# Key rows in the jobs' slots, a fourth such slot, loads three jobs ahead, and the first half's denominators during the contraction over tokens

## The chip, the cores and the metric

The kernel runs on one core of a Trainium2 chip. The metric is the device time of one execution in microseconds (us); shown are the median and the spread of several runs, and one execution taken by the hardware profiler, from which every row of a trace comes. Engines are named as in the profile: PE (TensorE; PEld its weight loads), DVE (VectorE), ACT (ScalarE), POOL (GpSimd) and SP (SyncE, which here only issues DMAs).

## What is computed

One linear-attention block on the layer norm of x, multiplied with a SwiGLU block on x itself, for 2048 tokens and 1024 channels in float32:

```
xn  = layernorm(x)
q, k, v = split(xn @ wqkv)            # 32 heads of 32
pq, pk  = phi(q), phi(k)              # phi(t) = (t+1 if t > 0 else exp(t)) + 1e-6
kv  = einsum("bhsd,bhse->bhde", pk, v)          # contraction over tokens
z   = sum of pk over tokens
o   = einsum("bhqd,bhde->bhqe", pq, kv) / (pq . z + 1e-6)
s   = o @ wo
g   = silu((silu(x @ w1) * (x @ w3)) @ w2)      # F = 3584
out = x + s * g
```

## The kernel before, in words

**Products.** Every float32 operand is split into a high and a low part in fp32r (`split`: a cast on ACT, L93, then a subtraction on DVE, L94), and every product is three matmuls of 128x512 (`mm3`, L101 to L103). Large products are done in 2 x 2 blocks with seven block products instead of eight (`gemm`). The names of a gemm's results a, b, c, d and of its sums u, c21, c12, c22 appear in the trace with a letter for the stage: ak is a of a key gemm, cg of a gate gemm. The weights' seven operands (B11, T2, T3, T1, B21, T4, B22) are made one after another from a loaded block (`Operands.made`; subtractions in L344), each in a tile of tag "b".

**Stages.** The tokens are worked in two halves of 1024. In order: preparation and keys of half 0, its q, its 28 gate and up gemms; keys of half 1; the contraction over tokens for both halves (`row_products`); q of half 1; gate and up of half 1; then the attention's output product (tiles with s in their names) and five layers of the second SwiGLU product (tiles with B).

**Keys.** For each result block of a key gemm `key_rows.use` makes phi (two activations on ACT, L497 and L498, then a DVE instruction, L499, that also gives the row sums for z, collected in `zacc` by L520) and appends a transposition to the list `later`. `turn` transposes the block on PE (tile trk, L505), copies it to a row tile (L506) and stores it to DRAM (`y_d`, L509, POOL's queue). A pair of key blocks has four row tiles: one of tag "c" and three more in two tiles of tag "b" (L529). `sums` adds their combinations on POOL.

**Contraction.** `row_products` has seven products of four steps each. A step loads 1 MB of x rows and key rows into a "raw" tile (L560, L562), for the last product also a second operand (yy, 0.5 MB, in a job slot), which POOL subtracts (L573); it splits them into four tiles of tag "b" and issues 24 matmuls (2 parts x 4 blocks x 3; tile g). A step's load is issued two steps ahead, its splits one step ahead. `row_sums` combines the results and stores them to `g_d` (L622, POOL's queue).

**Jobs.** Work that fills gaps is written as generators. `catch_up` pops one entry of `later`, or else advances the first generator of the list `jobs` by one yield; it is called six times in a gemm and twice in a step of the contraction. `tc.issue_after(m)` places what is issued inside it behind instruction m in the queue of m's engine; it orders nothing on other engines. In a gemm the first call carries a mark on ACT alone, the others one on ACT and one on DVE. `go_on` runs a list of jobs, with the loads of the next two issued ahead (L817). A job's tile comes from tag "job" with three slots of 4 KB a partition (`job_tile`, L121).

- `next_work`, during half 0: four jobs (`prepare_next`) that normalise the rows of half 1 and store its operands, with job tiles and one tile of tag "xg" (L258), and then sums of the w2 blocks (loads, POOL and DVE sums L755 to L769, stores L776).
- `attention_work`, during q, gate and up of half 1: first `spread_z` (block-diagonal `zb` in a "b" slot, L796 to L799; `zc` by L805), the denominators of half 0 (eight jobs; load L831, four matmuls L840 each, a reciprocal, and a store to `r_d`), then for each pair of wo blocks the key-value products (loads L892 of g_d and L894, matmuls L902) and the product with wo (load L917), the quotients of half 0, the denominators of half 1, and the quotients up to token block LATE = 6. A quotient (`divide`) loads pq and the reciprocals (L865, L867), waits three yields, multiplies on DVE (L873), adds block sums, and stores to `qs_d` (L877, L878), which the output product loads (L1128).
- What is left of a job list at the end of a half is run through there, without marks.

A scheduler sets the final order on each engine; the engines' queues are in order. Pools that matter: "b" with eight slots of 4 KB a partition, "raw" with two of 8 KB, "job" with three, PSUM with eight banks.

Of the kernel before, what the change touches and what calls it, by code (L numbers as in the profile page):

```python
# [16 lines left out]
P = 128  # L17
# [5 lines left out]
def tile_linear_attention_times_swiglu(  # L23
# [74 lines left out]
    def mm3(acc, w, a, start, stop):  # L98

        (wh, wl), (ah, al) = w, a  # L100
        nc.tensor.matmul(acc, lhsT=wh, rhs=ah, start=start, stop=False, skip_group_check=True)  # L101
        nc.tensor.matmul(acc, lhsT=wh, rhs=al, start=False, stop=False, skip_group_check=True)  # L102
        nc.tensor.matmul(acc, lhsT=wl, rhs=ah, start=False, stop=stop, skip_group_check=True)  # L103

# [15 lines left out]
    def job_tile(shape, name):  # L120
        return praw.tile(shape, F32, tag="job", bufs=3, name=name)  # L121

# [98 lines left out]
    def prepare_next(i):  # L221
# [8 lines left out]
        def steps(_):  # L230
# [26 lines left out]
            keep_rows(1, i, "A22", a22)  # L257
            g = st.tile([P, 2, C], F32, tag="xg", bufs=1, name=f"xg{i}")  # L258
            nc.gpsimd.tensor_add(out=g[:, 0], in0=a21, in1=a22)
            nc.gpsimd.tensor_sub(out=g[:, 1], in0=a11, in1=a21)  # L260
            yield True
            keep_rows(1, i, "S1", g.rearrange("p n c -> p (n c)"))
            for _ in range(3):
                yield True
            nc.gpsimd.tensor_sub(out=g[:, 0], in0=g[:, 0], in1=a11)
            nc.gpsimd.tensor_sub(out=g[:, 1], in0=a12, in1=g[:, 0])
            yield True
            keep_rows(1, i, "S2", g.rearrange("p n c -> p (n c)"))
            yield True
            p_ = turn("A11", a11)  # L270
            keep("A11", p_)
            nc.scalar.copy(out=a11, in_=p_)
            yield True
            p_ = turn("A21", a21)
            nc.scalar.copy(out=a21, in_=p_)
            yield True
# [234 lines left out]
    def key_rows(h, pair):  # L511
# [12 lines left out]
        def turn(n, c, pk):  # L524
            if (c, n) == (0, 0):
                t = rows[c, n] = small(f"y00_{h}_{pair}")
            else:
                if (1 - c, 1) not in pairs:
                    pairs[1 - c, 1] = pb.tile([P, 2, C], F32, tag="b", name=f"y{c}_{h}_{pair}")  # L529
                t = rows[c, n] = pairs[1 - c, 1][:, n if c else 0]  # L530
# [17 lines left out]
    def row_products():  # L548
# [39 lines left out]
        for at, s in enumerate(steps):  # L588
# [15 lines left out]
            for e, (x_, y_) in enumerate(split_.pop(s)):  # L604
                for m in M:
                    c = slice(m * P, (m + 1) * P)
                    mm3(b[m], (x_[:, 0, c], x_[:, 1, c]), (y_[:, 0], y_[:, 1]),
                        begins and e == 0 and not onto, ends and e == 1)
                    if ends and e == 1:
                        row_sums(i, m, b[m], u, v)  # L610
                catch_up()
                yield
# [31 lines left out]
    def half(h):  # L644
# [5 lines left out]
        def run(g):  # L650
            for _ in g:
                pass
# [32 lines left out]
        else:  # L685
            side_by_side(keys(0, paired=True), keys(1, paired=True))
            for pair in range(2, ND // 2):
                run(keys(pair))
            for _ in row_products():
                pass  # L690
# [125 lines left out]

    def go_on(work):  # L817

        data = [j.load() for j in work[:2]]
        for i, j in enumerate(work):  # L820
            yield from j.steps(data[i])
            if i + 2 < len(work):
                data.append(work[i + 2].load())

# [30 lines left out]
    def divide(m, k):  # L855
# [14 lines left out]
        def steps(t):  # L870
            for _ in range(3):
                yield True
# [80 lines left out]
    def late_work():  # L953
        yield from go_on([divide(m, k) for m in range(LATE, S // (2 * P)) for k in range(ND // 2)])

    def attention_work():
        yield from spread_z()
        H0, H1 = range(NCH // 2), range(NCH // 2, NCH)
        work = [j for c in H0 for j in denominators(c)]
        for k in range(ND // 2):  # L960
# [4 lines left out]
        work += [divide(m, k) for m in range(NT * H1[0], LATE) for k in range(ND // 2)]  # L965
        yield from go_on(work)

# [321 lines left out]
```

## Time and profile before

| | us |
|---|---|
| median of 3 runs | 2396.59 (2396.53 to 2399.76) |
| profiled execution | 2399.34 |
| its span in the trace | 2397.6 |
| key gemms of half 1 | about 752 to 855 |
| contraction over tokens | about 855 to 1015 |
| q, gate and up of half 1 | about 1015 to 1673 |

The profile's page gives the busy time of each engine as a share of the span, the costliest groups of instructions, and the chain of work that ended last. Its views on the trace are groups by line and tile, waits (who waited for whose instruction, in total us, times, longest), the timeline of an engine (start, duration, engine, line, operation, out<-in, and in brackets the idle time before it with what ended it), and stretches of time with the busy time of each engine in the order PE, PEld, DVE, ACT, POOL, then the granted clock of PE, the busy share of the DMA engines and GB/s. PE's busy time is modelled from pipelined matmuls; what it lost is read from the distance between the starts of matmuls and from its waits.

### The profile page before, as it was taken

What the parts mean: (1) busy time and instruction counts of PE and PEld (TensorE: products, weight loads), DVE (VectorE), ACT (ScalarE), POOL (GpSimd) and SP (SyncE); (2) the same over time, 40 slices, a digit from 0 to 9 for tenths busy, and PEclk for the clock granted to TensorE, in tenths of its full rate; (3) what the DMA queues carried; (4) which work ended last, traced back from release to release, by engine and by line L of the source; (5) the groups of instructions that cost most, each with busy time, mean ns of one, the idle gap of its engine ahead of it and who ended that gap; (6) DMA issues with size and microseconds to landing.
All of it is one profiled execution on the core that took longest, in us unless ns stands there. A gap on an engine that the chain in (4) does not pass through costs nothing.

```text
span 2397.6 us, 30961 instructions
## 1 busy us (share of the span) xinstructions
PE 2315.7 (97%) x10368; PEld 1896.1 (79%) x10368; DVE 1772.2 (74%) x2781; ACT 919.6 (38%) x1639; POOL 751.0 (31%) x892
## 2 busy tenths in 40 slices
PE   6999999999999889999999899999999999999998
PEld 5888788888887778778888788877787888888876
DVE  8878888887887655576766677777855676767798
ACT  5555333433332444344333233223423543342433
POOL 5341534367875320211423434323321000000033
PEclk9999999999999999999999999999999999999999
DMA  6455455476669566754555555557876665766588
GB/s 237 150 171 185 152 177 185 158 227 198 220 226 355 184 195 211 241 176 141 170 169 171 186 178 184 172 166 215 268 235 210 195 208 157 234 201 187 185 262 262
DMA packets 354016, 479.70 MB, mean 200 GB/s; under 512 B 24144, under 2 KB 262736, under 8 KB 353744
## 3 DMA queue, kind: packets, MB, share of 16 engines
q1 hardware_dynamic: 316608, 359.20, 47.8%
q0 software_dynamic: 37248, 118.52, 14.7%
q8 instruction: 81, 1.33, 0.2%
q14 instruction: 79, 0.65, 0.1%
HBM read 308.81 MB, written 172.49 MB: 201 GB/s over the span
## 4 chain that ended last, share of the span: by engine, by line
PE 43%; issue 10%; DMA 7%; DVE 4%; POOL 3%; ACT 1%; SPq 0%; POOLq 0%; DVEq 0%; ACTq 0%
PE g L101 2%; PE g L102 2%; PE g L103 2%; DMA qd<-pq_d 1%; PE cB L101 1%; PE cB L103 1%; PE cB L102 1%; PE aB L101 1%; PE aB L102 1%; PE dB L101 1%; PE aB L103 1%; PE dB L103 1%; PE dB L102 1%; DMA qs_d<-qd 1%; DMA rA22B<-h_d 1%
## 5 line engine op out<-in xcount | busy, mean ns | idle before, releaser
L740 POOL DMA_DIRECT2D h_d<-sg x112 | 82.7, 739 | 272.4 <-DVE sg L736 223.5
L1056 POOL DMA_DIRECT2D u_d<-uB x32 | 17.3, 540 | 407.1 <-DVE uB L1039 381.1
L94 DVE TENSOR_TENSOR xy<-xy,xy 128x512 fp32r<-128x512 f32 x112 | 75.9, 720 | 69.5 <-ACT xy L93 69.2
L93 ACT CAST xy<-xy 128x512 fp32r<-128x512 f32 x112 | 63.9, 620 | 86.2 <-PE g L103 60.1
L102 PE MATMUL g<-xy,xy 128*128 128x512 f32 x224 | 88.5, 395 | 0.0
L103 PE MATMUL g<-xy,xy 128*128 128x512 f32 x224 | 88.1, 394 | 0.0
L101 PE MATMUL g<-xy,xy 128*128 128x512 f32 x224 | 83.0, 395 | 2.8 <-ACT xy L93 2.3
L1039 DVE TENSOR_TENSOR acc<-cB,acc 128x512 f32<-128x512 f32 x50 | 34.3, 687 | 41.0 <-PE cB L103 41.0
L509 POOL DMA_DIRECT2D y_d<-y x40 | 29.7, 751 | 102.5 <-ACT y L506 79.7
L1039 DVE TENSOR_TENSOR acc<-dB,acc 128x512 f32<-128x512 f32 x56 | 38.5, 687 | 29.8 <-PE dB L103 29.6
L877 POOL DMA_DIRECT2D qs_d<-qd x32 | 17.9, 560 | 132.2 <-DVE qd L873 122.2
L722 POOL TENSOR_TENSOR hs<-sg 128x256 f32<-128x256 f32 x56 | 57.0, 1017 | 0.0
L720 POOL TENSOR_TENSOR hs<-hs,sg 128x256 f32<-128x256 f32 x56 | 56.4, 1008 | 0.1
L723 POOL TENSOR_TENSOR hs<-sg,hs 128x256 f32<-128x256 f32 x56 | 55.5, 992 | 1.6
L873 DVE SCALAR_TENSOR_TENSOR qd<-qd 128x512 f32<-128x512 f32 x32 | 21.9, 684 | 42.4 <-DMA qd<-pq_d 42.4
L101 PEld LDWEIGHTS g<-xy,xy 128*128 128x128 f32 x224 | 42.2, 189 | 12.5 <-ACT xy L93 2.9
L719 POOL TENSOR_TENSOR hs<-sg,sg 128x256 f32<-128x256 f32 x56 | 50.0, 892 | 1.2
L698 POOL DMA_DIRECT2D pq_d<-pq x32 | 17.4, 545 | 104.7 <-DVE pq L499 104.7
L102 PEld LDWEIGHTS g<-xy,xy 128*128 128x128 f32 x224 | 42.9, 192 | 9.0
L103 PEld LDWEIGHTS g<-xy,xy 128*128 128x128 f32 x224 | 42.9, 192 | 9.0
L748 POOL DMA_DIRECT2D h_d<-hs x60 | 45.9, 766 | 3.7 <-POOL hs L723 2.1
L755 POOL TENSOR_TENSOR w<-w 128x256 f32<-128x256 f32 x28 | 26.7, 955 | 58.5 <-DMA w<-in_B_w 58.5
(5311 smaller groups left out, 8383.7 us busy)
## 6 DMA issues: line engine op xcount, KB each, us to landing
h_d<-hs POOLq DMA_DIRECT2D x60, 256.0 KB, 3.3
h_d<-sg POOLq DMA_DIRECT2D x56, 256.0 KB, 3.5
w<-in_B_w SPq DMA_DIRECT2D x56, 256.0 KB
wt_d<-w SPq DMA_DIRECT2D x28, 512.0 KB
xy<-x_d SPq DMA_DIRECT2D x28, 512.0 KB
xy<-y_d SPq DMA_DIRECT2D x28, 512.0 KB
h_d<-hs SPq DMA_DIRECT2D x52, 256.0 KB
qs_d<-qd POOLq DMA_DIRECT2D x32, 384.0 KB, 4.6
```

Source lines behind the costliest of these rows:

```text
L93: nc.scalar.copy(out=hi, in_=src)
L94: return nc.vector.tensor_sub(out=lo, in0=src, in1=hi.bitcast(F32))
L101: nc.tensor.matmul(acc, lhsT=wh, rhs=ah, start=start, stop=False, skip_group_check=True)
L102: nc.tensor.matmul(acc, lhsT=wh, rhs=al, start=False, stop=False, skip_group_check=True)
L103: nc.tensor.matmul(acc, lhsT=wl, rhs=ah, start=False, stop=stop, skip_group_check=True)
L719: e.tensor_add(out=s1, in0=a21, in1=a22)
L720: e.tensor_sub(out=s2, in0=s1, in1=a11)
L722: e.tensor_sub(out=s3, in0=a11, in1=a21)
L723: e.tensor_sub(out=s4, in0=a12, in1=s2)
L740: nc.gpsimd.dma_start(out=h_d[i][2 * h + c][:, 2 * n:4 * n + 2, k], in_=src)
L748: queue.dma_start(out=h_d[i][2 * h + c][:, 6 + 4 * e:10 + 4 * e, k], in_=o[e].rearrange("p (e s) -> p e s", s=P))
L1039: return V.tensor_add(out=c, in0=src, in1=c)
```

## The change

- Tag "job" has four slots instead of three, and the tile "xg" becomes a job tile.
- `prepare_next` transposes the block A21 earlier and has three yields less for each of its four jobs.
- The two row tiles of a key pair come from the job slots instead of tag "b".
- `spread_z` and the denominators of half 0 become a job list of their own (`first_denominators`), which is appended before `row_products` and so runs in the contraction's calls of `catch_up`.
- These calls now stand behind the last matmul of their part of the step (`mm3` returns it).
- `attention_work` begins with the key-value products, and issues the loads of the next three jobs ahead.
- `divide` waits four yields instead of three for token blocks below LATE.

The number of instructions is the same.

```diff
@@ mm3
-        nc.tensor.matmul(acc, lhsT=wl, rhs=ah, start=False, stop=stop, skip_group_check=True)
+        return nc.tensor.matmul(acc, lhsT=wl, rhs=ah, start=False, stop=stop, skip_group_check=True)
@@ job_tile
-        return praw.tile(shape, F32, tag="job", bufs=3, name=name)
+        return praw.tile(shape, F32, tag="job", bufs=4, name=name)
@@ prepare_next
-            g = st.tile([P, 2, C], F32, tag="xg", bufs=1, name=f"xg{i}")
+            g = job_tile([P, 2, C], f"xg{i}")
             nc.gpsimd.tensor_add(out=g[:, 0], in0=a21, in1=a22)
             nc.gpsimd.tensor_sub(out=g[:, 1], in0=a11, in1=a21)
             yield True
             keep_rows(1, i, "S1", g.rearrange("p n c -> p (n c)"))
-            for _ in range(3):
-                yield True
+            p_ = turn("A21", a21)
+            nc.scalar.copy(out=a21, in_=p_)
+            yield True
+            yield True
             nc.gpsimd.tensor_sub(out=g[:, 0], in0=g[:, 0], in1=a11)
             nc.gpsimd.tensor_sub(out=g[:, 1], in0=a12, in1=g[:, 0])
             yield True
             keep_rows(1, i, "S2", g.rearrange("p n c -> p (n c)"))
-            yield True
             p_ = turn("A11", a11)
             keep("A11", p_)
             nc.scalar.copy(out=a11, in_=p_)
-            yield True
-            p_ = turn("A21", a21)
-            nc.scalar.copy(out=a21, in_=p_)
             yield True
@@ key_rows.turn
-                    pairs[1 - c, 1] = pb.tile([P, 2, C], F32, tag="b", name=f"y{c}_{h}_{pair}")
+                    pairs[1 - c, 1] = job_tile([P, 2, C], f"y{c}_{h}_{pair}")
@@ row_products
-                    mm3(b[m], (x_[:, 0, c], x_[:, 1, c]), (y_[:, 0], y_[:, 1]),
-                        begins and e == 0 and not onto, ends and e == 1)
+                    last = mm3(b[m], (x_[:, 0, c], x_[:, 1, c]), (y_[:, 0], y_[:, 1]),
+                               begins and e == 0 and not onto, ends and e == 1)
                     if ends and e == 1:
                         row_sums(i, m, b[m], u, v)
-                catch_up()
+                with tc.issue_after(last.ins):
+                    catch_up()
                 yield
@@ half
+            jobs.append((first_denominators(), False))
             for _ in row_products():
                 pass
@@ go_on
-    def go_on(work):
-        data = [j.load() for j in work[:2]]
+    def go_on(work, ahead=2):
+        data = [j.load() for j in work[:ahead]]
         for i, j in enumerate(work):
             yield from j.steps(data[i])
-            if i + 2 < len(work):
-                data.append(work[i + 2].load())
+            if i + ahead < len(work):
+                data.append(work[i + ahead].load())
@@ divide.steps
-            for _ in range(3):
+            for _ in range(4 if m < LATE else 3):
                 yield True
@@
+    H0, H1 = range(NCH // 2), range(NCH // 2, NCH)
+
+    def first_denominators():
+        yield from spread_z()
+        yield from go_on([j for c in H0 for j in denominators(c)])
+
     def attention_work():
-        yield from spread_z()
-        H0, H1 = range(NCH // 2), range(NCH // 2, NCH)
-        work = [j for c in H0 for j in denominators(c)]
+        work = []
         for k in range(ND // 2):
             for e, j in enumerate(merge_wo(k)):
                 work += key_values(k + e * (ND // 2)) + [j]
         work += [divide(NT * c + g, k) for c in H0 for g in range(NT) for k in range(ND // 2)]
         work += [j for c in H1 for j in denominators(c)]
         work += [divide(m, k) for m in range(NT * H1[0], LATE) for k in range(ND // 2)]
-        yield from go_on(work)
+        yield from go_on(work, 3)
```

## The prediction

> **What bounds the kernel now.** I read the page first: the busy shares and the chain of work that ended last.
>
> ```profile
> span 2397.6 us, 30961 instructions
> PE 2315.7 (97%) x10368; PEld 1896.1 (79%) x10368; DVE 1772.2 (74%) x2781; ACT 919.6 (38%) x1639; POOL 751.0 (31%) x892
> PE 43%; issue 10%; DMA 7%; DVE 4%; POOL 3%; ACT 1%; SPq 0%; POOLq 0%; DVEq 0%; ACTq 0%
> ```
>
> TensorE is busy for 97% of the span. The change keeps all 16618 instructions of the program (the compiled queues of both kernels, counted), so it can only take away or add idle time of PE. The second view is therefore the waits of PE, one row for each pair of waiting and releasing tile (columns: total us, times, longest).
>
> ```profile
> PE trk L505 <- DVE pk L499: 11.7, 4, 6.7
> PE cg__11115 L101 <- DVE c22g__11150 L462: 6.2, 1, 6.2
> PE B11s L101 <- ACT XA11s L93: 3.7, 1, 3.7
> PE g L101 <- ACT xy L93: 2.3, 1, 2.3
> PE bk__6485 L101 <- ACT T2k__6324 L93: 2.0, 1, 2.0
> PE cg__13351 L101 <- DVE c22g__13386 L462: 1.8, 1, 1.8
> PE B21s L101 <- ACT XA12s L93: 1.7, 1, 1.7
> PE bk__6485 L103 <- DVE T2k__6324 L94: 1.1, 1, 1.1
> PE ak__6979 L101 <- ACT uk__6978 L439: 1.2, 1, 1.2
> PE aq__8368 L101 <- ACT uq__8367 L439: 0.7, 1, 0.7
> ```
>
> These ten rows add up to 32.4 us. They are the waits near the edited code: the keys of the second half, the contraction over tokens, the start of q, and the division by the denominators. That is the whole stake, 1.4% of the span; the start (0 to 75 us) and the last layers keep their order of instructions.
>
> The third view is the timeline of PE, which shows what a wait costs beyond itself (columns: start, us, engine, line, operation, idle before and its releaser).
>
> ```profile
> 757.75 0.39 PE L102 MATMUL ak__6468<-A,B11k__6258 128*128 128x512 f32 x1
> 757.98 0.39 PE L103 MATMUL ak__6468<-A,B11k__6258 128*128 128x512 f32 x1
> 760.41 0.50 PE L101 MATMUL bk__6485<-S,T2k__6324 128*128 128x512 f32 x1 [2.04 <-ACT T2k__6324 L93]
> 762.27 0.64 PE L103 MATMUL bk__6485<-S,T2k__6324 128*128 128x512 f32 x1 [1.14 <-DVE T2k__6324 L94]
> 765.70 0.49 PE L102 MATMUL bk__6485<-S,T2k__6324 128*128 128x512 f32 x1
> ...
> 825.21 0.63 PE L505 MATMUL trk<-ident,pk 128*128 128x128 f32 x4 [2.26 <-DVE pk L499]
> ...
> 1007.52 1.52 PE L101 MATMUL g<-xy,xy 128*128 128x512 f32 x4 [2.33 <-ACT xy L93]
> 1011.75 0.39 PE L103 MATMUL g<-xy,xy 128*128 128x512 f32 x1
> ```
>
> Undisturbed matmuls start 0.23 us apart (757.75, 757.98). From 762.27 to 765.70 there are eight intervals, 3.43 us, where 8 x 0.23 makes 1.8: after the wait PE ran slowly for another 1.6 us. From 1007.52 to 1011.75 eleven intervals take 4.23 us, 1.7 too many. I call this the slow start. Beside it stands a rule that would size it otherwise: the Trainium skill, TensorE: Matmul & The Clock Gate, part 1 on the clock gate, says that the array falls to half clock after at least one idle window of about 3.4 us. By it alone the waits of 2.0 and 2.3 us would have had no slow start, and the sum below would lose 3.3 us of its gain; the trace shows the slow start after both, so here the measurement decides.
>
> **The change, part by part.** All of it goes against the profiled execution, 2399.34 us around a span of 2397.6; the median of the runs is 2396.59, 2.75 us lower, and I put the sum onto that median.
>
> *Job slots 3 to 4, transposes of the layer-norm rows earlier, three steps fewer in each of the four preparing jobs.* In the changed program's queues the sums of the w2 blocks end before the second half's keys; before, they still ran there, with their stores.
>
> ```profile
> 740.12 0.76 SPq L324 DMA_DIRECT2D wk__6237<-in_A_wqkv  x1
> 752.63 0.62 ACT L93 CAST B11k__6258<-wk__6237 128x512 fp32r<-128x512 f32 x1 [3.43 <-DMA wk__6237<-in_A_wqkv]
> 756.24 2.26 DVE L344 TENSOR_TENSOR wk__6218<-wk__6218 128x512 f32<-128x512 f32 x1
> 758.43 0.68 DVE L344 TENSOR_TENSOR wk__6237<-wk__6237 128x512 f32<-128x512 f32 x1
> 720.00:780.00 60.00, 56.82 (x243) 46.25 (x242) 41.64 (x50) 16.89 (x28) 31.88 (x39) 0.97 1.01 358
> 900.00:960.00 60.00, 60.00 (x266) 49.69 (x266) 33.35 (x53) 27.35 (x49) 2.18 (x4) 1.00 0.66 211
> ```
>
> The key weights issued at 740.12 were used at 752.63, in a stretch where DMA was full (share 1.01, 358 GB/s, last columns of the stretches) and POOL busy for 31.88 us; one subtraction took 2.26 us where its sister took 0.68. T2k came late, and PE lost 2.0 + 1.1 + 1.6. The w2 traffic and POOL's sums leave this place. I take 3.5 of the 4.7 us (bounds 0 and 4.7). **-3.5**
>
> *Key rows in the jobs' places.* The eight slots of tag b then hold weight operands only, and the splits of the next key block run earlier. The wait at 825 (2.26) and the following one of ak (1.2) came from DVE being late between such splits: 3.4 us, I take 2.7. **-2.7** (0 to -3.4). But what is early now stands in front of something.
>
> ```profile
> 800.64 0.63 PE L505 MATMUL trk<-ident,pk 128*128 128x128 f32 x4 [2.42 <-DVE pk L499]
> 848.39 3.72 ACT L93 CAST xy<-xy 128x512 fp32r<-128x512 f32 x7
> 854.95 1.12 PE L505 MATMUL trk<-ident,pk 128*128 128x128 f32 x4 [6.66 <-DVE pk L499]
> ```
>
> At 800.64 PE waits for phi of the third block. In the new queue of ACT three casts (T4, B22 and the next B11), a copy and two negations more stand ahead of the first exponential: six operations of 0.53 us (3.72 / 7). **+3.2** (0 to +5). At 854.95 it is the other way round: seven casts of x and y lay between the copies and phi of the last block; the new queue has two there. Five times 0.53: **-2.7** (0 to -5).
>
> *Denominators of the first half during the contraction.* Their loads leave the end of the contraction and the start of q.
>
> ```profile
> 994.51 0.37 SPq L562 DMA_DIRECT2D xy<-x_d  x1
> 998.79 0.57 SPq L831 DMA_DIRECT2D pqd<-pq_d  x1
> 1003.00 0.62 ACT L93 CAST xy<-xy 128x512 fp32r<-128x512 f32 x1 [2.54 <-DMA xy<-x_d]
> ```
>
> The x rows issued at 994.51 were there at 1003.00, 8.5 us later, with pq loads and weights around them; then PE waited (2.3, slow start 1.7, and 0.7 for aq): 4.7 us, I take 3.9. **-3.9** (0 to -4.7). They arrive elsewhere: eight pq loads and four second operands for the last product (0.5 MB each) now lie between the first and the third product, with eight steps of 1 MB. That is 14 MB in 211 matmuls x 0.227 = 48 us, at most 292 GB/s, between the 211 and the 358 of the two stretches. zb takes one of the eight slots from the steps' four operand tiles each; a load can then start about half a step (12 matmuls, 2.7 us) later. Counting back over three steps of 24 matmuls (16.3 us) less 2.5 for casts and subtractions, a landing may take 13.8 us with eight slots, 11.1 with seven; 8.5 was measured. So it should hold: **+2** for a hitch (0 to +15, priced under the rivals). The first denominator follows its load by 24 matmuls (5.4 us), and zb is ready one matmul ahead: **+1.5** (0 to +4). The two additions, reciprocals and small stores of r stand among the splits on DVE and on a POOL that is idle there (2.18 us of 60): nothing. The new marks behind the last matmul order only PE's own instructions there, no other queue: nothing.
>
> *Key-value products at once.* Without denominators ahead, the first one stands 35 matmuls (7.9 us) behind the contraction's end, and its operand comes through DRAM from the last block.
>
> ```profile
> 1014.74 0.39 PE L101 MATMUL aq__8368<-A,B11q__8319 128*128 128x512 f32 x1
> 1018.90 0.54 POOL L622 DMA_DIRECT2D g_d<-gc  x1 [1.05 <-DVE eps L802]
> DMA to landing us min/median/max: 2.3/4.1/8.5
> ```
>
> (The last row is that of the tile g_d.) The last store went out at 1018.90, 4.2 us after q's first matmul at 1014.74; zb's and eps' instructions are gone from DVE there, so say 3.8. Then 4.1 to landing, and about 3 for the load that waits for it: an estimate of mine below the 8.5 us that the twice as large x rows took among other loads, since no row has this one. 10.9 us after the end against 7.9. PE's queue is in order, so the rest of q's first block waits behind it; on SP, which waits for the store, only loads of later jobs stand behind, since the next weights of q are issued ahead. **+4** with some slow start (0 to +7).
>
> *Loads three ahead, four waiting steps in divide.* This view is DVE and SP of the same stretches.
>
> ```profile
> 1363.97 0.69 DVE L873 SCALAR_TENSOR_TENSOR qd<-qd 128x512 f32<-128x512 f32 x1 [7.58 <-DMA qd<-pq_d]
> L873 DVE SCALAR_TENSOR_TENSOR qd<-qd 128x512 f32<-128x512 f32 x32 | 21.9, 684 | 42.4 <-DMA qd<-pq_d 42.4
> 1348.44 0.50 PE L101 MATMUL cu__10947<-A,T4u__10980 128*128 128x512 f32 x1 [0.60 <-DVE c22u__10977 L462]
> 1670.11 0.80 SPq L1128 DMA_DIRECT2D r0q<-qs_d  x2
> ```
>
> DVE waited 42.4 us in nine places for these loads, but PE felt three: cg__11115 (6.2), cg__13351 (1.8) and 0.60 at 1348. In the new queues six of the 32 stay within 21 matmuls of their load. The one behind the 6.2 is among them: its slot is released at the same distance, 45 matmuls against 46. I give it 1.2 back, 0.3 at cg__13351, all of the 0.60: **-2.1** (0 to -8.6). The attention's first operands, loaded at 1670.11 behind the last quotient's store, and released to PE at B11s (3.7) and B21s (1.7), are issued 32 matmuls earlier (7.3 us): 5.4 us and a slow start of 1.6, I take 5.5. **-5.5** (0 to -7). With 208 steps against 201 for 192 places, seven more steps are left over for the end of the second half, as a bunch of DVE work; I see no PE wait in it.
>
> Sum: -3.5 - 2.7 + 3.2 - 2.7 - 3.9 + 2 + 1.5 + 4 - 2.1 - 5.5 = **-9.7**. That is 2389.6 beside the profiled 2399.34, and 2386.9 beside the median: **2387 us**. Instructions shift in the first half's gate and up stage as well, where one wait like T2k's could come or go: I give that 4 us to either side.
>
> **The rivals.**
>
> *The contraction starves (slower).* Between its first and third product every step's load competes with a pq or yy load, with seven slots. If a landing passes 11 us, the step pays what 1007.52 paid: 2.3 + 1.7 = 4.0 us. Five of the eight steps would cost 20 us where the sum has 2, and make 2405. For it: the 12.5 us from 740.12 to 752.63 in the full stretch. Against it: 292 GB/s is not full, 8.5 us was landed beside pq loads before, and the steps there have no subtraction on POOL. The rule on the ceiling bears on this: the Trainium skill, DMA: Bandwidth & Descriptors, under Bandwidth, puts the HBM limit of one core at about 358 GB/s, which the 358 in the full stretch agrees with; by it 14 MB need 39 of the 48 us, and the mean doesn't starve.
>
> *The gains are eaten (no change).* The waits at 760 and at 1673 stay for half (+4.5), and the key-value wait takes the longest landing, 8.5 instead of 4.1 (+4.4): 2396. For it: each wait has a second producer close behind, as the waits of trk show.
>
> *The change gives more.* The wait at 800 doesn't grow (-3.2), the key-values are in time (-4), the 6.2 goes as well (-5): 2375.
>
> **How the numbers follow.** Forecast (2380 to 2392) 0.45; starving (2398 to 2415) 0.20; eaten (2392 to 2398) 0.22; more (below 2380) 0.13. A difference below 0.2%, 4.8 us, is about what cannot be told from none here. Faster takes the forecast and the third: 0.58; within 0.2% 0.23; slower 0.19. The range leaves out the lower half of the last case and the upper end of the starving: 2375 to 2406.
>
> **What would show it.** Right: no PE wait for T2k near 760; trk's waits near 800 longer, near 855 about 4 us; xy no releaser of PE at the contraction's end; kv with a wait of about 3 us released by gw; B11s without one. Wrong: several rows g <- xy in the first three products, or the sum of PE's waits unchanged with other names.

## The result and the profile after

The changed kernel takes 2420.95 us (median of 4 runs, 2417.23 to 2428.7); the kernel before, in the same comparison, 2398.18. The ratio is 1.0097, with a 95% interval of 1.0069 to 1.0126: slower by 23 us, where 10 us less were forecast, and outside the range. The profiled execution of the changed kernel is the slowest of its four, 2428.7 us. Executions of one kernel differ by some 10 us here, so I read a whole from its median only.

The page of the changed kernel first: the span, the busy time of the engines, and the engines' shares of the chain that ended last.

```profile
span 2426.6 us, 30936 instructions
PE 2325.3 (96%) x10368; PEld 1903.0 (78%) x10368; DVE 1802.1 (74%) x2781; ACT 921.9 (38%) x1639; POOL 748.2 (31%) x892
PE 70%; DVE 11%; DMA 8%; issue 6%; ACT 2%; POOL 1%; SPq 0%; POOLq 0%; DVEq 0%; ACTq 0%
```

PE, DVE, ACT and POOL have as many instructions as before. DVE's share of the chain went from 4% to 11%: PE waits for DVE more than before. Which waits these are, the view of PE's waits on the changed kernel tells (total us, times, longest).

```profile
PE trk L503 <- DVE pk L497: 10.9, 3, 5.7
PE cg__13349 L101 <- DVE c22g__13379 L460: 9.6, 1, 9.6
PE kv L902 <- DMA gw<-g_d: 5.1, 1, 5.1
PE as L101 <- ACT us L1091: 4.7, 1, 4.7
...
PE cg__3948 L101 <- DVE c22g__3982 L460: 4.1, 1, 4.1
PE cg__2328 L101 <- DVE c22g__2366 L460: 3.8, 1, 3.8
PE cg__2974 L101 <- DVE c22g__3012 L460: 3.8, 1, 3.8
PE cg__3620 L101 <- DVE c22g__3658 L460: 3.7, 1, 3.7
...
PE g L101 <- ACT gu L625: 2.7, 1, 2.7
PE cs L101 <- DVE s L1050: 2.4, 1, 2.4
...
PE cg__2656 L101 <- DVE c22g__2690 L460: 1.7, 1, 1.7
...
PE cg__3302 L101 <- DVE c22g__3336 L460: 1.5, 1, 1.5
...
PE bk__6485 L103 <- DVE T2k__6337 L94: 0.6, 1, 0.6
...
PE bk__6485 L101 <- ACT T2k__6337 L93: 0.5, 1, 0.5
...
PE g L101 <- ACT xy L93: 0.2, 1, 0.2
```

Six rows of cg, 18.6 us, lie in the first half's gate and up gemms (numbers 2328 to 3948), a stage that the prediction had left with "4 us to either side". The kernel before had three waits of 4.4 us there, and one of 1.8 us in the output product:

```profile
PE dg__2322 L101 <- DVE c22g__2353 L468: 2.6, 1, 2.6
PE cg__4230 L101 <- DVE c22g__4264 L462: 1.0, 1, 1.0
PE cu__3107 L101 <- DVE c22u__3139 L462: 0.8, 1, 0.8
...
PE ds L101 <- DVE s L1039: 1.8, 1, 1.8
```

One new wait of cg, 9.6, ends the second half's gate and up. B11s is gone, g for xy is down to 0.2 us and T2k to 1.1. But the output product now waits 4.7 us in as and 2.4 in cs.

Where the time went, by stage. A stage runs from the start of the first matmul of its tile in the trace to that of the next (ak, aq, ag for the two halves, g for the contraction, as for the attention's output product, B11B for the layers); keys 0 begins with the span, and the layers end with the last matmul's start. The rows B11s to B22s ahead of as count to gate/up 1. In us, one profiled execution each.

| kernel | keys 0 | q 0 | gate/up 0 | keys 1 | contraction | q 1 | gate/up 1 | output | layers |
|---|---|---|---|---|---|---|---|---|---|
| before | 127.4 | 79.2 | 546.2 | 103.0 | 159.0 | 86.5 | 605.0 | 136.3 | 544.4 |
| after | 131.0 | 79.2 | 567.8 | 96.6 | 167.2 | 92.1 | 591.8 | 144.2 | 543.8 |
| e1 | 130.7 | 79.6 | 543.4 | 105.8 | 169.3 | 92.8 | 590.5 | 144.4 | 544.7 |
| e2 | 128.4 | 81.2 | 562.3 | 103.0 | 156.7 | 88.5 | 604.2 | 136.1 | 545.6 |
| e3 | 128.9 | 79.2 | 551.5 | 95.4 | 168.6 | 92.9 | 590.3 | 143.0 | 544.7 |
| e4 | 129.1 | 79.6 | 544.8 | 105.0 | 168.8 | 93.4 | 577.6 | 141.4 | 544.3 |
| e5 | 131.0 | 79.6 | 543.1 | 105.7 | 164.8 | 83.5 | 579.9 | 145.0 | 544.3 |
| e6 | 127.3 | 79.2 | 556.9 | 97.0 | 165.2 | 91.2 | 577.6 | 142.7 | 540.9 |
| e7 | 128.6 | 79.2 | 550.5 | 106.1 | 168.2 | 91.7 | 577.6 | 143.0 | 543.8 |
| e8 | 128.6 | 79.2 | 544.7 | 106.8 | 162.2 | 92.5 | 577.6 | 142.0 | 542.1 |
| e9 | 128.5 | 79.2 | 545.1 | 106.6 | 163.0 | 83.5 | 579.6 | 141.6 | 543.3 |
| e10 | 128.6 | 79.2 | 544.7 | 108.5 | 163.2 | 83.5 | 580.4 | 143.6 | 545.4 |
| e11 | 128.9 | 79.2 | 544.9 | 106.5 | 162.4 | 83.5 | 581.4 | 141.4 | 545.1 |
| e12 | 132.6 | 79.2 | 551.6 | 97.4 | 163.6 | 83.5 | 579.6 | 142.7 | 544.4 |
| e13 | 128.7 | 79.2 | 544.5 | 108.5 | 163.1 | 76.2 | 612.1 | 135.7 | 543.6 |
| e14 | 128.9 | 79.2 | 557.6 | 96.5 | 168.5 | 93.2 | 592.0 | 142.9 | 546.6 |
| e15 | 128.8 | 79.2 | 555.5 | 96.4 | 165.5 | 83.5 | 579.3 | 143.7 | 544.1 |

(Denominators' matmuls move from the second half's q and gate/up to the contraction, and key-value matmuls between q and gate/up; so these three are to be added up where work moves. Stages with the same code differ between the profiles by up to 3 us in gate/up 0, 543.1 to 546.2 with the preparing steps of before, and by up to 6 in keys 0 and the layers; smaller differences are not read by themselves. A profiled execution lies up to 8 us from the median of its kernel: after 7.8 above it, e6 6.0 below.) After against before: +21.6 in gate/up 0, -6.4 in the keys of the second half, and +8.5 from the contraction to the output product together.

Now the first of these losses in detail. DVE's timeline in the changed kernel, around two of the four preparing jobs:

```profile
248.84 3.46 DVE L736 TENSOR_TENSOR sg<-c21u__2257,sg 128x512 f32<-128x512 f32 x1
252.22 0.68 DVE L489 TENSOR_TENSOR c12u__2285<-du__2156,uu__2134 128x512 f32<-128x512 f32 x1
...
262.34 2.17 DVE L94 TENSOR_TENSOR T2u__2344<-wu__2129,T2u__2344 128x512 fp32r<-128x512 f32 x1 [0.75 <-ACT T2u__2344 L93]
...
266.10 0.68 DVE L460 TENSOR_TENSOR c22g__2366<-cg__2328,ug__2302 128x512 f32<-128x512 f32 x1
...
334.55 3.46 DVE L736 TENSOR_TENSOR sg<-c21u__2903,sg 128x512 f32<-128x512 f32 x1
```

and POOL's and PE's beside the first:

```profile
249.20 1.30 POOL L259 TENSOR_TENSOR xg<-xn 128x512 f32<-128x512 f32 x1
250.45 1.29 POOL L260 TENSOR_TENSOR xg<-xn,xn 128x512 f32<-128x512 f32 x1
252.59 0.73 POOL L740 DMA_DIRECT2D h_d<-sg  x1 [0.85 <-DVE sg L736]
253.35 1.21 POOL L719 TENSOR_TENSOR hs<-sg,sg 128x256 f32<-128x256 f32 x1
254.53 1.18 POOL L722 TENSOR_TENSOR hs<-sg 128x256 f32<-128x256 f32 x1
```

```profile
266.83 0.58 PE L101 MATMUL cg__2328<-A,T4g__2241 128*128 128x512 f32 x1 [3.84 <-DVE c22g__2366 L460]
```

The DVE instruction L736 takes 3.46 us instead of 0.68: it ends at 252.30, 0.56 us behind the two POOL sums (251.74). POOL's sums of sg (L719 on) then start late and lie beside DVE's next subtractions (2.17 us for T2u), and c22g comes 3.8 us too late for PE. In the next job the same instruction takes the same 3.46 us, 85.7 us later (334.55). The Trainium skill, SBUF — State Buffer, on the two separate sides, describes such a hold: a DVE operation with two SBUF inputs and a GpSimd operation that reads SBUF lock the same pair of ports for a whole instruction, and the one that starts second waits. That L736 ends about its own 0.68 us behind the second sum agrees with that. Its record starts 0.36 us ahead of the first sum (248.84 against 249.20), so the trace does not show which of the two came first.

The second loss, at the end of gate/up 1; DVE's timeline there in the changed kernel:

```profile
1645.71 0.69 DVE L873 SCALAR_TENSOR_TENSOR qd<-qd 128x512 f32<-128x512 f32 x1 [4.99 <-DMA qd<-pq_d]
...
1659.90 0.69 DVE L873 SCALAR_TENSOR_TENSOR qd<-qd 128x512 f32<-128x512 f32 x1 [4.54 <-DMA qd<-pq_d]
...
1674.04 0.69 DVE L873 SCALAR_TENSOR_TENSOR qd<-qd 128x512 f32<-128x512 f32 x1 [2.00 <-DMA qd<-pq_d]
...
1677.44 0.68 DVE L460 TENSOR_TENSOR c22g__13379<-cg__13349,ug__13330 128x512 f32<-128x512 f32 x1
```

DVE stands idle at three quotients until their loads land, 11.5 us in 30, and c22g comes behind them.

The third: SP's waits in the changed kernel between 875 and 910 us, at the start of the contraction.

```profile
SPq L558 <- DMA y_d<-y: 6.1, 1, 6.1
SPq L560 <- DVE eps L802: 6.0, 1, 6.0
SPq L831 <- DMA y_d<-y: 4.6, 2, 3.1
```

and what came of it, on ACT and PE:

```profile
902.89 0.62 ACT L93 CAST xy<-xy 128x512 fp32r<-128x512 f32 x1 [4.40 <-DMA xy<-x_d]
903.41 2.04 ACT L625 COPY gu<-g 128x512 f32<-128x512 f32 x4
```

```profile
904.04 0.50 PE L101 MATMUL g<-xy,xy 128*128 128x512 f32 x1 [2.69 <-ACT gu L625]
```

The denominators' loads (L831, the third row) wait for job slots that hold key rows until their stores have landed; SP's queue is in order, so the x rows behind them are late, ACT waits 4.40 us for these, and the copy gu behind that cast is what PE needs. Waits like the first two rows stand in e8 as well (7.8 and 6.5 us), where the third row and the wait for gu are gone.

### The profile page after: what moved, and what is told of

It is laid out like the page before. It is cut to its first block, busy times and chain, and to the rows that moved or that the text cites. A ratio compares the mean times of both kernels' runs of the same rounds, so it can differ in the third digit from the quotient of the medians.

```text
span 2426.6 us, 30936 instructions
## 1 busy us (share of the span) xinstructions
PE 2325.3 (96%) x10368; PEld 1903.0 (78%) x10368; DVE 1802.1 (74%) x2781; ACT 921.9 (38%) x1639; POOL 748.2 (31%) x892
## 4 chain that ended last, share of the span: by engine, by line
PE 70%; DVE 11%; DMA 8%; issue 6%; ACT 2%; POOL 1%; SPq 0%; POOLq 0%; DVEq 0%; ACTq 0%
PE g L101 1%; PE g L103 1%; PE g L102 1%; PE cB L101 1%; PE aB L101 1%; PE cB L102 1%; PE cB L103 1%; PE aB L102 1%; PE dB L101 1%; PE aB L103 1%; PE dB L102 1%; PE dB L103 1%; DMA qd<-pq_d 1%; DMA rA22B<-h_d 1%; DVE sg L736 1%
## 5 line engine op out<-in xcount | busy, mean ns | idle before, releaser
L1060 POOL DMA_DIRECT2D u_d<-uB x32 | 17.3, 542 | 407.8 <-DVE uB L1043 383.9
L94 DVE TENSOR_TENSOR xy<-xy,xy 128x512 fp32r<-128x512 f32 x112 | 81.1, 759 | 68.2 <-ACT xy L93 68.0
L698 POOL DMA_DIRECT2D pq_d<-pq x32 | 17.6, 549 | 111.7 <-DVE pq L497 103.0
L719 POOL TENSOR_TENSOR hs<-sg,sg 128x256 f32<-128x256 f32 x56 | 51.4, 917 | 1.2
L1174 POOL DMA_DIRECT2D s_d<-s x32 | 17.5, 546 | 85.6 <-DVE s L1043 56.9
```

The lines of the kernel that those rows point to most:

```text
L94: return nc.vector.tensor_sub(out=lo, in0=src, in1=hi.bitcast(F32))
L719: e.tensor_add(out=s1, in0=a21, in1=a22)
```

## The experiments

Theory A, formed from the trace: the preparing job's steps went from 27 to 24, four gemms of six calls, so the same heavy step (normalising, POOL's sums) meets the same place of a gemm in all four jobs, and a bad one. Its rival, B: the row tile in a job slot, or the earlier transposition, does it. For the end of gate/up 1: the fourth waiting step. Each ratio stands against the kernel before in the same comparison. There are four comparisons (e1 to e4, e5 to e8, e9 to e12, e13 to e15); between runs of different ones the ratios say more than the medians.

**e1: the preparing steps of before, in the changed kernel** (27 steps, A21 last).

```diff
-            p_ = turn("A21", a21)
-            nc.scalar.copy(out=a21, in_=p_)
-            yield True
-            yield True
+            for _ in range(3):
+                yield True
...
             keep_rows(1, i, "S2", g.rearrange("p n c -> p (n c)"))
+            yield True
             p_ = turn("A11", a11)
...
+            p_ = turn("A21", a21)
+            nc.scalar.copy(out=a21, in_=p_)
+            yield True
```

> The changed kernel with the preparing jobs' steps as before (27 steps each, A21 transposed last), everything else changed. Theory A (the 24 steps are four gemms of six calls, so the same heavy step meets the same place of a gate gemm in all four jobs): the waits of cg for c22g between 260 and 490 us fall from about 19 us to the 5 of before, and the time falls by some 20 us, to about 2400. Rival B (the row sums' tile in a job slot, or the fourth slot, delays POOL there): the waits stay and the time stays near 2420. The waits at the end of the gate and up stage (9.8 us near 1678) stay under both.

2414.53 us (ratio 1.0069, 1.0054 to 1.0084). Gate/up 0 falls to 543.4, so B's job slot is not it; but the whole gains only 6.4 us by the medians, since the keys of the second half lose their gain again (105.8). The wait at the end of gate/up 1 stays.

**e2: those steps alone, in the kernel before**, the reverse of e1's edit, with three slots and the old tile.

```diff
-            for _ in range(3):
-                yield True
+            p_ = turn("A21", a21)
+            nc.scalar.copy(out=a21, in_=p_)
+            yield True
+            yield True
```

> The kernel before with nothing changed but the preparing jobs' steps (24 each, A21 transposed early; its own tile, three job slots). Theory A: four waits or more of cg for c22g, about 4 us each, every 85 us from 265, 15 us lost there; the weight sums end sooner, which gives back up to 5 near 760: 2405 to 2415. Rival B: no new waits, at or below the kernel before, 2390 to 2398.

2421.62 us (1.0102, 1.0081 to 1.0122): above the range of A and against B. Gate/up 0 takes 562.3, 16.1 more than before, with the same three waits of 3.7 to 3.8 us (tiles cg__2328, cg__2974, cg__3620). The gain that was expected near 760 did not come: keys 1 stays at 103.0. Alone, this part costs as much as the whole change.

**e3: the 24-step jobs, begun three calls later.**

```diff
     def next_work():
 
+        for _ in range(3):
+            yield True
         yield from go_on([prepare_next(i) for i in range(TH // 2)])
```

> The changed kernel with three idle steps ahead of the first preparing job: still 24 steps a job, but half a gemm later. Theory A with a bad place: the heavy step now falls three products later, the waits of cg for c22g at 266, 352 and 438 go or become something else, 2400 to 2410. If it is the 24 steps or the order of the steps as such, whatever the place: the same four waits appear shifted by about 9 us, and the time stays near 2420.

2408.53 us (1.0046, 1.0032 to 1.0061). Gate/up 0 at 551.5, 16 less than after: the place counts. In place of the four waits of cg of 3.7 to 4.1 us stand three of 2.4 us of dg and three of 1.0 to 1.4 of cg. The keys keep their 95.4.

**e4: e1 with three waiting steps in the quotients.**

```diff
-            for _ in range(4 if m < LATE else 3):
+            for _ in range(3):
                 yield True
```

> As e1 with three waiting steps in the quotients instead of four (201 steps of attention work; loads still three ahead). If the four steps, which leave more of the job over for the end of the stage, make the 9.8 us wait of cg near 1678: that wait shrinks to below 3 us and the time is some 7 us below e1. If it comes from the loads three ahead or from the stage's end as such: same as e1 within 3 us, while the shorter distance brings back waits of DVE for qd in the middle of the stage.

2397.25 us (1.0003, 0.9993 to 1.0013): 17.3 below e1, more than twice the expected 7. The long wait of cg (9.1 us in e1) is gone; gate/up 1 is 12.9 shorter, the output product 3.0. (The attention work of e4 has 184 steps for 192 calls, not 201: 17 have moved into the contraction. The changed kernel's 208 leave 16 over.)

**e5: e4 with the denominators from the third product on, and the key-values four steps later.**

```diff
-            jobs.append((first_denominators(), False))
             for _ in row_products():
...
             begins, ends = s[1:] == ks[0], s[1:] == ks[-1]
+            if begins and i == 2:
+                jobs.append((first_denominators(), False))
...
+        for _ in range(4):
+            yield True
         yield from go_on(work, 3)
```

> As e4 with two moves that act in different stages: the first half's denominators begin with the third product of the contraction instead of the first, and four idle steps stand ahead of the key-value products. If the pq loads among the first product's steps delay x and with it the copy gu, for which PE waits 4 us there: that wait goes and the contraction is about 4 us shorter than in e4 (168.8 to about 165). If seven slots do it, a like wait comes at another boundary. The wait of kv for gw (5.1 us) goes, q is 5 to 6 us shorter (93.4 to about 88). Both: about 2388.

2386.98 us (0.9955, 0.9938 to 0.9972), as expected. The contraction falls by 4.0 (the wait for gu from 4.1 to 1.1), q 1 by 9.9, of which 2.3 come back in gate/up 1 (moved work).

**e6: e4 with 24 preparing steps in the old order.**

```diff
-            for _ in range(3):
+            for _ in range(2):
                 yield True
             nc.gpsimd.tensor_sub(out=g[:, 0], in0=g[:, 0], in1=a11)
...
             keep_rows(1, i, "S2", g.rearrange("p n c -> p (n c)"))
-            yield True
...
             keep("S4", a12)
-            yield True
```

> As e4, the preparing jobs in their old order with three idle steps taken out: 24 steps each. Theory A (24 steps lock the heavy steps to one place of the gate gemm): gate and up of the first half grows from 544.8 to about 560, with the wait of cg or dg four times, 85 us apart, total about 2408. Rival (the early A21 transposition does the harm): stage stays at 545, and the keys of the second half get shorter by about 9 as the weight sums end sooner: about 2390.

2397.41 us (1.0002, 0.999 to 1.0013). Gate/up 0 grows to 556.9, with these waits of PE among others:

```profile
PE cg__2328 L101 <- DVE c22g__2360 L460: 2.6, 1, 2.6
PE cg__2974 L101 <- DVE c22g__3006 L460: 2.6, 1, 2.6
PE cg__3620 L101 <- DVE c22g__3652 L460: 2.6, 1, 2.6
```

The same three tiles as after, without the early transposition: the 24 steps are enough for 12.1 us. The hold is there, too: L736 takes 3.45 us at 245.10, 329.10 and 412.97. It does so three times in the changed kernel and in e2 as well, and over 3 us in no other kernel's gate/up 0 but once in e7. With the new order the 24 steps cost twice as much (24.4 us from e1 to the changed kernel), so the order, with its early transposition, counts as well. The total of 2408 was missed, because the keys of the second half fall from 105.0 to 97.0 at the same time; gain and loss cancel.

**e7: the changed kernel's order filled up to 27 steps, three waiting steps in the quotients.**

```diff
             keep("S4", a12)
-            yield True
+            for _ in range(4):
+                yield True
```

> The changed kernel with three waiting steps in the quotients, and the new order of the preparing steps filled up to 28 by four idle ones at each job's end, so that neighbouring jobs fall four calls apart. Theory A: the bad place comes at most in two of the four jobs; gate and up of the first half at 548 to 554, total about 2400. Rival (the early transposition): about 560, total about 2410.

2399.61 us (1.0013, 1.0001 to 1.0025), gate/up 0 at 550.5: as A has it. The edit puts four idle steps in place of one, so that a job has 27 steps, not 28, and neighbouring jobs fall three calls apart. The waits of cg near 267, 353 and 438 are gone, so the new order does not make the loss whatever the number of steps; at 24 steps it has a share (e6). A wait of 4.0 us near 504 (cg__4237) makes most of the 5.7 us over e4; its cause is open. Keys 1 is at 106.1, as in e1 and e4.

**e8: e4 with the key rows back in tag b.**

```diff
-                    pairs[1 - c, 1] = job_tile([P, 2, C], f"y{c}_{h}_{pair}")
+                    pairs[1 - c, 1] = pb.tile([P, 2, C], F32, tag="b", name=f"y{c}_{h}_{pair}")
```

> As e4 with the key rows back in tag b; the job slots stay four. If the key rows in the job slots hold the splits free as predicted, the keys of the second half grow here from 105 us towards 108 or more. If they gain nothing without the earlier end of the weight sums, the stage stays at 103 to 105 and the first half's keys are 1 to 2 us shorter (129.1 to 127.4): 2394 to 2397.

2388.2 us (0.9957, 0.9941 to 0.9973), 9 below e4 by the medians and 11 by the ratios, which neither expectation had. Keys 1 hardly changes (106.8), the contraction falls from 168.8 to 162.2: the wait for gu is gone, since the job slots are free for the denominators' loads.

**e9: e8 with the key-values four steps later.**

```diff
+        for _ in range(4):
+            yield True
         yield from go_on(work, 3)
```

> As e8 (key rows in tag b, old preparing steps, three waiting steps in the quotients) with four idle steps ahead of the key-value products. The wait of kv for gw (4.8 us) and its slow start go: q of the second half from 92.5 to about 84, median about 2381. If the wait only moves to the next operands (wo, or kv of the next block), q stays above 88 and the time within 3 us of e8.

2384.07 us (0.9945, 0.9928 to 0.9962). The wait of kv is gone; q 1 falls by 9.0, gate/up 1 grows by 2.0.

**e10: e9 with loads two jobs ahead.**

```diff
-        yield from go_on(work, 3)
+        yield from go_on(work, 2)
```

> As e9 with the loads two jobs ahead, as before the change, instead of three. If the third load ahead is what removed the waits of DVE for qd that PE felt (6.4 us near 1374 before): gate and up of the second half grows from 577 by 5 to 10 us, with that wait back. If the room in the list (184 steps and 4 idle ones for 192 calls, nothing left over) did it: the stage grows by less than 3.

2383.92 us (0.9949, 0.993 to 0.9968): the same as e9. The quotients' groups on DVE, e9 first and then e10 (busy, mean ns, idle before):

```profile
L875 DVE SCALAR_TENSOR_TENSOR qd<-qd 128x512 f32<-128x512 f32 x32 | 21.8, 683 | 6.9 <-DMA qd<-pq_d 6.9
```

```profile
L875 DVE SCALAR_TENSOR_TENSOR qd<-qd 128x512 f32<-128x512 f32 x32 | 21.8, 682 | 7.0 <-DMA qd<-pq_d 7.0
```

With two ahead as with three, DVE waits once, 7 us instead of 42.4 before: the third load ahead gives nothing here.

**e11: e9 with four idle steps ahead of the late quotients.**

```diff
     def late_work():
+        for _ in range(4):
+            yield True
```

> As e9 with four idle steps ahead of the late quotients, which are loaded during the attention's output product. If their loads stand in the way of that product's operands (cs waits 4 us for a sum behind the operand XS3s): the wait goes and the stage from as to B falls from 142 to about 137. If the operands are late for another reason: the stage stays at 141 to 145.

2383.43 us (0.9943, 0.9928 to 0.9959); the output product stays at 141.4. The late quotients' loads are not what makes it 5 us longer than before the change; that stays open.

**e12: all parts but the fourth waiting step, moved in time**: the changed kernel with e3's and e4's edits and those of e5.

```diff
+        for _ in range(3):
+            yield True
         yield from go_on([prepare_next(i) for i in range(TH // 2)])
...
-            for _ in range(4 if m < LATE else 3):
+            for _ in range(3):
...
-            jobs.append((first_denominators(), False))
...
+            if begins and i == 2:
+                jobs.append((first_denominators(), False))
...
+        for _ in range(4):
+            yield True
         yield from go_on(work, 3)
```

> All parts of the change but the fourth waiting step, each put elsewhere in time: preparing jobs of 24 steps begun three calls later, key rows in the job slots, denominators from the third product on, four idle steps ahead of the key-values. By the stages of e3 and e5: gate and up of the first half 551, keys of the second 95, contraction 165, q 84, gate and up 579: about 2384. If the stages' gains do not add, 2390 or more.

2389.39 us (0.9966, 0.9951 to 0.998): 5 above the expected. Its stages came as expected to within 3 us, except the first half's keys (132.6); so the later place keeps the keys' gain (97.4) at a price of 6 us in gate/up 0, and no more is won than by e9.

**e13: e9 with 24 idle steps ahead of the key-values instead of four.**

```diff
-        for _ in range(4):
+        for _ in range(24):
             yield True
         yield from go_on(work, 3)
```

> As e9 with 24 idle steps ahead of the key-values instead of 4: 208 steps for 192 calls, so 16 are left over at the end of the stage as in the changed kernel, but the quotients wait three steps as before. If the left-over steps make the loss: a wait of cg of 8 to 10 us returns at the end of gate and up, the stage and the output product together are 12 to 17 us longer than in e9, median near 2398. If the fourth waiting step itself does: within 4 us of e9.

2405.56 us (1.003, 1.0017 to 1.0043), 21 above e9 with three waiting steps in the quotients. PE's waits in it, and one row of DVE:

```profile
PE B11s L101 <- ACT XA11s L93: 16.6, 1, 16.6
...
PE cu__13480 L101 <- DVE c22u__13517 L462: 6.1, 1, 6.1
```

```profile
1686.40 0.69 DVE L875 SCALAR_TENSOR_TENSOR qd<-qd 128x512 f32<-128x512 f32 x1 [4.56 <-DMA qd<-pq_d]
```

So 16 steps left over at the stage's end, as in the changed kernel, make such a loss with three waiting steps too. That the fourth wait costs nothing by itself is not shown: no run has four waits and nothing left over. The 20 further idle steps also put the whole list later; that the loss lies at its end is read from these rows. The loss falls on another tile (the output product's first operand) than expected.

**e14: the changed kernel with the two sums of rows on DVE.**

```diff
-            nc.gpsimd.tensor_add(out=g[:, 0], in0=a21, in1=a22)
-            nc.gpsimd.tensor_sub(out=g[:, 1], in0=a11, in1=a21)
+            nc.vector.tensor_add(out=g[:, 0], in0=a21, in1=a22)
+            nc.vector.tensor_sub(out=g[:, 1], in0=a11, in1=a21)
```

> The changed kernel with the two sums of rows at L259 and L260 on DVE instead of POOL. If the DVE instruction held beside them (3.46 us) starts the delay: DVE has two instructions of 0.68 more but is not held, the three waits of 4 us of cg for c22g shrink below 2, and gate and up of the first half falls from 567.8 to 552 to 558; median near 2408. If the delay comes from POOL's other sums (L719 to L723) being late for another reason, or from the transposition: stage at 565 or more.

2414.83 us (1.0073, 1.0049 to 1.0097). Gate/up 0 falls by 10.2 to 557.6. DVE's timeline and PE's waits in e14:

```profile
246.66 0.68 DVE L736 TENSOR_TENSOR sg<-c21u__2257,sg 128x512 f32<-128x512 f32 x1
247.26 0.68 DVE L259 TENSOR_TENSOR xg<-xn 128x512 f32<-128x512 f32 x1
247.86 2.50 DVE L260 TENSOR_TENSOR xg<-xn,xn 128x512 f32<-128x512 f32 x1
```

```profile
PE cg__2656 L101 <- DVE c22g__2690 L460: 2.5, 1, 2.5
PE cg__3302 L101 <- DVE c22g__3336 L460: 2.4, 1, 2.4
PE cg__2328 L101 <- DVE c22g__2366 L460: 2.2, 1, 2.2
...
PE cg__2974 L101 <- DVE c22g__3012 L460: 2.2, 1, 2.2
```

L736 is back at 0.68, so POOL's two sums held it. Three waits fall from 3.8 to 2.2, not below 2, and two rise (cg__2656 from 1.7 to 2.5, cg__3302 from 1.5 to 2.4). About half of the loss, 10.2 us, hangs on the two sums being on POOL; how much of that is the hold, and how much POOL's next sums being late, is not separated. And the hold has moved: on DVE L260 takes 2.50 us and ends at 250.36, 0.56 us behind two sums of POOL (249.80).

```profile
248.36 0.75 POOL L719 TENSOR_TENSOR hs<-sg,sg 128x256 f32<-128x256 f32 x1
249.06 0.74 POOL L722 TENSOR_TENSOR hs<-sg 128x256 f32<-128x256 f32 x1
```

**e15: e12 without the three idle steps, the sums on DVE** (e14's edit beside this one).

```diff
-        for _ in range(3):
-            yield True
         yield from go_on([prepare_next(i) for i in range(TH // 2)])
```

> As e12 without the three idle steps ahead of the preparing jobs, and with the two sums on DVE. If e14's idea holds: gate and up of the first half 550 to 556, everything else as in e12, 2385 to 2393. Without it: 565, about 2400.

2394.9 us (0.9992, 0.9979 to 1.0005), 2 above the expected range's end; gate/up 0 at 555.5. The later place (e12, 551.6) is worth more than the other engine.

## Why the prediction was wrong, point by point

- **"Instructions shift in the first half's gate and up stage as well ... 4 us to either side".** This step failed, and costs the most: 21.6 us between the profiles, 16.1 in e2, where the steps were changed alone. I had called ten waits near the edited code "the whole stake", but the preparing jobs, edited too, run in this stage. I had looked at the steps' number only for where the list ends, not for where each step falls in a gemm. e2 shows the loss from this part alone, e6 that 24 steps in the old order make half of it, e3 and e7 that it falls when the steps fall elsewhere. A DVE instruction held beside POOL's two sums goes with it (the changed kernel, e2, e6); with those sums on DVE about half of it goes (e14). What makes the rest is open.
- **"Seven more steps are left over ... I see no PE wait in it".** The second failed step: 9.6 us of wait, 17.3 us by the medians of e1 and e4, and 21 by those of e9 and e13. The steps left over run without marks, one quotient after another close behind its load, on a DVE that the last gemms need. It had to be read from the loads' distances, which I had counted for the middle of the stage only.
- **"5.4 us and a slow start of 1.6, I take 5.5"** for the attention's first operands. The waits B11s and B21s went, but the gain did not come: the output product behind them is 7.9 us longer (136.3 to 144.2), with waits of 4.7 and 2.4 us where before there was one of 1.8. It is 5 us longer in e9 too, and e11 did not find the cause.
- **The keys of the second half** (-3.5 - 2.7 + 3.2 - 2.7 = -5.7): measured -6.4. T2k's wait fell from 3.1 to 1.1, that near 800 grew from 2.4 to 5.7, that near 855 fell from 6.7 to 3.1. But I had given parts of this to each edit by itself, and neither has it alone, so that the sum came out is partly luck. Keys 1 takes 103.0 with the early weight sums alone (e2: POOL ends them at 733 us and the key gemms begin at 772; in the kernel before, the sums end at 783 and the gemms begin at 753). It takes 105.0 with the key rows in job slots alone (e4), and 95 to 97 with both (after, e3, e6).
- **The contraction** (+2 and +1.5 for a hitch and the first denominator): the wait for gu rose from 0.4 to 2.7 us. The mechanism was not the bandwidth that the starving rival asked about, nor the seventh slot: SP stood behind job slots full of key rows (e8: 6.6 us less in this stage).
- **The key-values** (+4): a wait of 5.1, released by gw as foretold. Without it (e9) q 1 is 9.0 us shorter, of which 2.0 come back in gate/up 1; by the ratios the whole gains 2.9 us on e8, within the intervals.
- **The waits that were to go** went: xy at the contraction's end (2.3 to 0.2), B11s, and the 6.2 us of cg__11115 too, which I had kept. e10 shows that the third load ahead did not do that. It may be the room that the moved denominators leave in the list; that is argued, not shown.
- **The rivals.** None was the one that came. The slower one had its place in the contraction; most of the loss was before and after it.

## What to carry to other kernels

Where side work is advanced by a fixed number of calls per tile of main work, a step count that is a multiple of it puts every job's heaviest step at the same place: count the steps modulo the calls, and look which engine has no room at that place. Count the calls against the steps of the whole list as well; what is left over runs in a bunch at the worst moment, and each added waiting step counts once for every job in the list. A buffer pool shared by two kinds of work ties their queues together: here a load waited for another's store, and everything behind it in the queue waited too. With the steps counted so (e9: key rows in b, 27 preparing steps, three waiting steps, key-values four calls later), what is left of the change is worth 0.55%.

## What the runs showed of the hardware that was not expected

One DVE instruction with both inputs in SBUF (L736, 128x512 f32, 0.68 us alone) was held by two POOL instructions in a row, 1.30 and 1.29 us, and did not get in between them: it took 3.46 us and ended 0.56 us behind the second. This came three times each in the changed kernel, e2 and e6 (3.45 or 3.46 us). And a kernel's executions spread differently: 2417.23 to 2428.7 for the changed one, 2382.79 to 2385.15 for e9; why is open.
